# A gated mix of softmax and linear attention on one core: the linear branch's feature map taken from a copy, two of its steps and the softmax scaling on GpSimd, and a new static order

## The chip, the core and the metric

The kernel runs on one core of a Trainium2 chip. The time is device microseconds of one execution; the figure is the median of several runs. A change of time below about 0.3% can't be told from none here.

Engines are named as in the profile: PE (TensorE), ACT (ScalarE), DVE (VectorE), POOL (GpSimd), SP (SyncE, which issues DMAs here). PEld is PE's weight load.

## What is computed

The input x is 2048 x 512 (bf16). Branch A is softmax attention with 32 heads of 16, branch B linear attention with as many; a sigmoid gate per row mixes them.

```python
def _A_ref(x, wqkv, wo):                 # H = 32, Dh = 16
    q, k, v = ...                        # x @ wqkv, split by head
    scores = jnp.einsum("bhqd,bhkd->bhqk", q, k) * (Dh ** -0.5)
    p = _softmax(scores, axis=-1)
    o = jnp.einsum("bhqk,bhkd->bhqd", p, v)
    return merge_heads(o) @ wo
def _B_ref(x, wqkv, wo):
    phi = lambda t: jnp.where(t > 0, t + 1, jnp.exp(t)) + 1e-6
    pq, pk = phi(q), phi(k)
    kv = jnp.einsum("bhsd,bhse->bhde", pk, v); z = jnp.einsum("bhsd->bhd", pk)
    o = einsum("bhqd,bhde->bhqe", pq, kv) / (einsum("bhqd,bhd->bhq", pq, z) + 1e-6)
    return merge_heads(o) @ wo
g = _sigmoid((x * gate_w).sum(-1, keepdims=True))
return g * a + (1 - g) * b
```

(`merge_heads` stands for the reference's transpose and reshape.)

## The kernel before, in words

**Units and rounds.** Branch A's scores are cut into units: one head, 128 keys, 512 queries, a 128x512 tile of PSUM. There are 32 rounds of 64 units, 2048 in all: a round is a group of eight heads (`t8`, four of them), a block of 512 queries (`qc`, four) and a parity (`par`, the even or the odd four of the eight heads). The four heads of a round sit in four row strips of PE, so up to four score matmuls go side by side (tiles `KT` and `Qz`). Their value matmuls sit in four column strips and all add up in one PSUM bank, bank 7 (weights `Vp` or `Vs`, 17 columns: 16 of V and one of ones, which gives the softmax's sum).

**Two ways to take the exponential.** A pair of units in banks 0-1 or 2-3 is read by one ACT exp of 128x1024 into a `P` tile (L894) and gives one value matmul ("piece") a unit. A unit in bank 4, 5 or 6 is drained by DVE: one addition and a maximum write an int16 tile `Z` whose bits, read as bf16, are a rough power of two (L806 drains banks 5 and 6 together, 128x1024; L845 drains one bank alone, 128x512). POOL adds two constants to its bits (`int64_add`, L871, twice for each pair), and the three tiles, weighted by `Vp` and the two scaled copies `Vs`, together approximate the exponential: three pieces a unit. A pair takes three of 18 `Z` buffers. Which unit goes which way is decided by the planner below.

**Tasks.** Everything else is a list of tasks with a release and a due time (`TS`), most of which take one of the banks 4, 5, 6 for a projection: keys, queries and values of A (`t_k`, `t_q`, `t_v`), scaling of the value weights (`t_vs`, L1136), the gate, and branch B: 16 tiles of phi(k) (`t_phik`), from them the products `MT`, `KVbd` and the sums `Zbd`, then 16 tiles of phi(q) (`t_phiq`), the denominators (`t_den`), B's output (`t_bout`) and the final projection (`t_final`).

**The feature map** (`phi`, L1197 to L1207) takes a 128x512 projection in bank b. ACT takes the exp from PSUM into `eb` (L1202, bf16), DVE makes min(e, 1) + 1e-6 in place (L1203), and DVE reads the bank again for max(t + 1 + 1e-6, e) into `phiK` (L1204). Only then is the bank free. There are two `eb` buffers.

**The end of a round** (`aout`): DVE transposes bank 7 into `T1` (L1164), which frees the bank for the next round. After every second round (15 times; the last pair is done in another way, L1174 to L1181) DVE takes the reciprocals of the sums (L1190), multiplies `T1` by them into `T2` (L1191), and transposes `T2` into `OAT` (L1194).

**What sets the order.** Every instruction's place on its engine is fixed when the kernel is built. A planner keeps, per engine, the time at which it would be free, with a planned duration of each operation (such as 606 for L845), and takes again and again the candidate that can start first, ties broken by priorities. L1203, L1191 and L1136 carry a mark (`_Port`) by which the planner lengthens them when they would meet a POOL instruction. 129 sets of knobs, one for each 16 units issued (`PLAN`, read by `X`), shift these priorities: how long PE waits for a fourth piece (`PWN`), which banks tasks may take (`B4`), and so on. The kernel then waits on semaphores only where the data need it; each engine takes its instructions in the written order. All matmuls are recorded on L482.

Of the kernel before, what the change touches and what calls it, by code (L numbers as in the profile page):

```python
# [7 lines left out]
ACT = mybir.ActivationFunctionType  # L8
# [107 lines left out]
LAT = 53.0  # L116
LATP = 97.0
LATS = 34.0
# [22 lines left out]
def bass_gated_mix__mha_block__linear_attn_block__prompt_kernel(  # L141
# [22 lines left out]
    def spl(t):  # L164
# [10 lines left out]
    DEF = {"SKEW": 4, "DSL": 80.0, "DTOL": 500.0, "PWE": 0.0, "PWT": 0.0, "PWN": 400.0, "TPR": 620, "RIDE": 1200.0, "HP": 115.0, "HD": 115.0, "NDB": 2, "SLK": 50.0, "UEX": 0.2, "TOP": 420, "B4": 1, "ROOM": 3, "REL": 0, "BOOT": 2, "PORT": 0, "LD": 8}  # L175
    PLAN = {
        0: {"UEX": -0.3, "TPR": 720, "PWE": 50.0},
        1: {"UEX": -0.3, "TPR": 720, "PWE": 50.0},
        2: {"UEX": -0.3, "TPR": 720, "PWE": 50.0, "HD": 300.0},
        3: {"UEX": -0.3, "TPR": 720, "PWE": 50.0, "HD": 300.0},  # L180
        4: {"UEX": -0.3, "TPR": 720, "PWE": 50.0, "HD": 60.0},
        5: {},
        6: {},
        7: {"UEX": -0.3, "TPR": 720, "PWE": 50.0},
        8: {"UEX": -0.3, "TPR": 720, "PWE": 50.0, "DSL": 0.0, "PWN": 200.0, "DTOL": 1000.0, "REL": 1.0, "ROOM": 4, "SLK": -100.0},
        9: {"REL": 1.0},
        10: {"REL": 1.0},
        11: {"REL": 0.5, "HD": 300.0, "PWN": 200.0, "ROOM": 1, "DSL": 0.0, "RIDE": 600.0},
        12: {"REL": 1.0, "HD": 300.0, "PWN": 200.0, "ROOM": 1, "DSL": 0.0, "RIDE": 600.0, "PWE": 100.0, "B4": 0},
        13: {"REL": 1.0, "HD": 0.0, "PWN": 200.0, "ROOM": 1, "DSL": 0.0, "RIDE": 600.0, "PWE": 100.0, "B4": 0},  # L190
        14: {"REL": 1.0},
        15: {"REL": 1.0, "PWN": 600.0},
        16: {"REL": 1.0, "PWN": 600.0},
        17: {"REL": 1.0, "HP": 220.0, "PWT": 400.0},
        18: {"REL": 1.0, "HP": 220.0, "PWT": 400.0},
        19: {"REL": 1.0, "HP": 160.0, "PWT": 400.0},
        20: {"REL": 1.0, "HP": 160.0, "PWT": 400.0},
        21: {"REL": 1.0, "HP": 160.0, "PWT": 400.0},
        22: {"REL": 1.0, "HP": 220.0, "PWT": 400.0, "PWE": 100.0, "B4": 2},
        23: {"REL": 0.5, "HP": 160.0, "PWT": 400.0, "PWN": 200.0},  # L200
        24: {"REL": 0.5, "HP": 160.0, "PWT": 400.0, "PWN": 200.0, "DTOL": 0.0, "HD": 200.0},
        25: {"REL": 1.0, "PWN": 600.0, "B4": 2},
        26: {"REL": 1.0, "PWE": 50.0, "DTOL": 0.0, "DSL": 300.0},
        27: {"REL": 1.0, "HP": 220.0, "PWT": 400.0, "HD": 60.0, "PWE": 200.0},
        28: {"REL": 1.0, "HP": 220.0, "PWT": 400.0, "HD": 60.0, "PWE": 200.0, "B4": 2},
        29: {"REL": 1.0, "HP": 220.0, "PWT": 400.0, "HD": 60.0, "PWE": 50.0},
        30: {"REL": 1.0, "HP": 220.0, "PWT": 400.0, "UEX": 1.0, "SKEW": 2},
        31: {"REL": 1.0, "HP": 220.0, "PWT": 400.0, "UEX": 1.0, "SKEW": 2, "RIDE": 300.0},
        32: {"REL": 1.0, "HP": 220.0, "UEX": 1.0, "HD": 60.0, "SKEW": 2, "RIDE": 900.0, "PORT": 1, "PWE": 100.0, "DSL": 300.0},
        33: {"REL": 1.0, "HP": 220.0, "PWT": 250.0, "UEX": 1.0, "HD": 200.0, "SKEW": 2, "RIDE": 900.0, "PWE": 100.0, "DSL": 300.0, "PWN": 600.0},  # L210
        34: {"HP": 160.0, "PWT": 250.0, "RIDE": 600.0, "PWN": 900.0, "SKEW": 2, "DSL": 0.0},
        35: {"SKEW": 0, "TPR": 450},
        36: {"SKEW": 0, "TPR": 450},
        37: {"SKEW": 0, "TPR": 560, "ROOM": 2, "PWN": 200.0, "HD": 200.0, "DSL": 150.0, "PWE": 200.0},
        38: {"SKEW": 0, "TPR": 560, "ROOM": 2, "PWN": 200.0, "HD": 200.0, "DSL": 150.0, "PWE": 200.0},
        39: {"REL": 1.0, "HP": 220.0, "PWT": 250.0},
        40: {"UEX": -0.3, "TPR": 720, "PWE": 50.0, "DSL": 0.0, "PWN": 200.0, "DTOL": 1000.0, "REL": 1.0, "ROOM": 4, "SLK": -100.0, "PWT": 400.0, "HP": 160.0},
        41: {"UEX": -0.3, "TPR": 720, "PWE": 50.0, "DSL": 0.0, "B4": 0, "PWN": 200.0, "DTOL": 1000.0, "REL": 1.0, "ROOM": 4, "SLK": -100.0, "PWT": 400.0, "HP": 160.0, "PORT": 1, "SKEW": 2},
        42: {},
        43: {"UEX": -0.3, "TPR": 560, "PWE": 50.0, "DSL": 0.0, "PWN": 200.0, "DTOL": 1000.0, "REL": 1.0, "ROOM": 1, "SLK": -100.0, "PWT": 250.0, "HP": 160.0, "PORT": 1, "SKEW": 2},  # L220
        44: {"UEX": -0.3, "TPR": 560, "PWE": 50.0, "DSL": 0.0, "PWN": 200.0, "DTOL": 1000.0, "REL": 1.0, "ROOM": 1, "SLK": -100.0, "PWT": 250.0, "HP": 160.0, "PORT": 1, "SKEW": 2},
        45: {"UEX": -0.3, "TPR": 560, "PWE": 50.0, "DSL": 0.0, "PWN": 200.0, "DTOL": 1000.0, "REL": 1.0, "ROOM": 1, "SLK": 0.0, "NDB": 1, "PWT": 250.0, "HP": 160.0, "PORT": 1, "SKEW": 2},
        46: {},
        47: {},
        48: {},
        49: {"HP": 160.0},
        50: {"HP": 160.0},
        51: {"HP": 160.0, "B4": 0, "SKEW": 1, "DTOL": 1000.0, "HD": 200.0},
        52: {"HP": 160.0},
        53: {"HP": 160.0, "DTOL": 1000.0},  # L230
        54: {"UEX": -0.3, "TPR": 720, "PWE": 50.0, "HD": 60.0},
        55: {"UEX": -0.3, "TPR": 720, "PWE": 50.0, "HD": 60.0, "SKEW": 1, "DTOL": 0.0, "DSL": 0.0},
        56: {"UEX": -0.3, "TPR": 720, "PWE": 50.0, "HD": 60.0, "SKEW": 1, "DTOL": 0.0, "DSL": 0.0, "RIDE": 300.0},
        57: {"UEX": -0.3, "TPR": 650, "PWE": 50.0, "HD": 60.0, "SKEW": 1, "REL": 1.0, "DTOL": 0.0, "DSL": 0.0, "RIDE": 300.0, "SLK": -100.0, "PWT": 100.0},
        58: {"UEX": -0.3, "TPR": 650, "PWE": 50.0, "SKEW": 1, "REL": 1.0, "DTOL": 2000.0, "DSL": 0.0, "RIDE": 300.0},
        59: {"HP": 160.0, "SKEW": 1},
        60: {"HP": 160.0, "SKEW": 1, "PWE": 50.0, "DTOL": 2000.0, "UEX": -0.3},
        61: {"REL": 1.0, "PWN": 600.0, "B4": 2, "DTOL": 2000.0},
        62: {"REL": 1.0, "PWN": 600.0, "B4": 2, "PWT": 250.0},
        63: {"REL": 1.0, "B4": 2, "HD": 200.0, "PWT": 250.0, "ROOM": 2},  # L240
        64: {"REL": 1.0, "B4": 2, "HD": 200.0, "PWT": 250.0, "ROOM": 2},
        65: {},
        66: {"UEX": -0.3, "TPR": 720, "PWE": 50.0},
        67: {"UEX": -0.3, "TPR": 720, "PWE": 50.0, "HD": 300.0, "RIDE": 300.0, "B4": 2},
        68: {"UEX": -0.3, "TPR": 650, "PWE": 50.0, "HD": 300.0, "RIDE": 300.0, "B4": 2, "ROOM": 2, "PWN": 600.0, "DTOL": 2000.0},
        69: {"UEX": -0.3, "TPR": 650, "PWE": 50.0, "HD": 300.0, "RIDE": 300.0, "B4": 2, "ROOM": 2, "PWN": 600.0, "DTOL": 2000.0, "REL": 0.5},
        70: {"REL": 1.0, "B4": 2, "HD": 200.0, "PWT": 250.0, "ROOM": 2, "HP": 160.0},
        71: {"REL": 1.0, "B4": 2, "HD": 200.0, "PWT": 250.0, "ROOM": 2, "HP": 160.0, "RIDE": 600.0},
        72: {"REL": 1.0, "B4": 2, "HD": 200.0, "PWT": 250.0, "ROOM": 2, "HP": 160.0, "RIDE": 2500.0, "UEX": 0.6},
        73: {"REL": 1.0, "PWN": 600.0, "B4": 2, "HD": 60.0, "PWT": 250.0, "ROOM": 2, "HP": 220.0, "RIDE": 2500.0},  # L250
        74: {"REL": 1.0, "PWN": 200.0, "B4": 2, "HD": 60.0, "PWT": 250.0, "HP": 220.0, "RIDE": 2500.0, "TPR": 650, "SLK": 0.0},
        75: {"REL": 1.0, "PWN": 200.0, "HD": 60.0, "PWT": 250.0, "HP": 220.0, "RIDE": 2500.0, "TPR": 650, "SLK": 0.0},
        76: {"REL": 1.0, "PWN": 200.0, "HD": 60.0, "PWT": 250.0, "HP": 220.0, "RIDE": 600.0, "TPR": 650, "SLK": 0.0, "SKEW": 1},
        77: {"UEX": -0.3, "TPR": 650, "PWE": 50.0, "HD": 60.0, "SKEW": 1, "TOP": 800, "REL": 1.0, "DTOL": 0.0, "DSL": 0.0, "RIDE": 300.0, "SLK": -100.0, "PWT": 100.0},
        78: {"UEX": 0.6, "TPR": 650, "PWE": 50.0, "HD": 60.0, "SKEW": 1, "TOP": 800, "REL": 1.0, "DTOL": 1000.0, "DSL": 0.0, "RIDE": 300.0, "SLK": -100.0, "PWT": 100.0},
        79: {"ROOM": 1, "PWN": 900.0, "REL": 1.0, "SKEW": 0},
        80: {"ROOM": 1, "PWN": 200.0, "REL": 1.0, "SKEW": 0, "DSL": 0.0, "HP": 220.0, "TPR": 650},
        81: {"REL": 1.0, "PWN": 600.0, "B4": 2, "DTOL": 2000.0, "PWT": 100.0},
        82: {"REL": 1.0, "B4": 0, "DTOL": 2000.0, "PWT": 100.0},
# [1372 lines left out]
```

## Time and profile before

| | |
|---|---|
| median of 3 runs | 655.76 us (655.49 to 657.0) |
| profiled execution | span 653.0 us from its first to its last instruction, granted TensorE clock 1.000; its time is not given apart from the span |
| ACT exps of scores (L894) | 664 of 128x1024: 1328 units |
| DVE drains (L806, L845) | 301 pairs and 118 singles: 720 units |
| POOL adds (L871) | 726, 437.5 us busy |
| feature map, 32 tiles | L1202 21.8 us on ACT; L1203 9.6 and L1204 22.0 us on DVE |
| normalisation, 15 times | L1191 12.3 us, L1190 5.1, L1194 10.5, all on DVE |
| scaling of value weights (L1136) | 32 times, 0.244 to 0.740 us, 14.5 us |

How to read it: a row of the groups gives line, engine, operation, output <- input, shapes and count, then busy time, the mean length of one in ns, and the engine's idle time just before them with what ended it. Busy times on PE are the union of overlapping matmuls in flight. On DVE, ACT and PE an instruction's length overlaps the next one's beginning, so the distance between two starts is what one takes of the engine. The chain is the sequence of work that ended last. In a timeline, the columns are start, length, engine, line, operation, tiles and count, and in brackets the idle time before it and what ended it.

### The profile page before, as it was taken

How to read it: one execution, taken by the hardware profiler on the slowest of the kernel's cores; microseconds unless marked ns; L12 is line 12 of the kernel's file. 1: busy time of each engine (PE TensorE's matmuls, PEld its weight loads, DVE VectorE, ACT ScalarE, POOL GpSimd, SP SyncE). 2: the span in 40 equal slices, each digit the busy share in tenths (PEclk: the TensorE clock that was granted, in tenths of full speed). 3: DMA queues.
4: the chain of work that ended last, by engine and by line, in shares of the span. 5: the costliest groups of instructions: out<-in, count | busy, mean ns of one | idle time of the engine just before them, and what ended most of it. 6: DMA issues, size and time to landing. Idle time of an engine off the chain costs nothing.

```text
span 653.0 us, 20046 instructions
## 1 busy us (share of the span) xinstructions
PE 631.8 (97%) x8601; PEld 191.1 (29%) x8601; DVE 582.2 (89%) x723; ACT 633.0 (97%) x706; POOL 442.7 (68%) x744
## 2 busy tenths in 40 slices
PE   8999999999999999999999999999999999999998
PEld 4422232322222223233333223222222222222224
DVE  6899989898798998899889899889999898998994
ACT  5899999999999999999999999999999999999995
POOL 4376576676687787676666456668678786877683
PEclk9999999999999999999999999999999999999999
DMA  7610001000100000000101000000000000001001
GB/s 162 188 27 4 8 1 34 2 2 11 34 10 2 2 15 6 11 2 2 34 9 26 19 11 9 14 21 16 20 10 19 26 18 26 10 17 27 17 3 34
DMA packets 33072, 14.82 MB, mean 23 GB/s; under 512 B 24404, under 2 KB 32980, under 8 KB 32984
## 3 DMA queue, kind: packets, MB, share of 16 engines
q1 hardware_dynamic: 31640, 13.01, 8.3%
q8 instruction: 69, 1.13, 0.7%
q10 hardware_dynamic: 1344, 0.52, 0.3%
q14 instruction: 19, 0.16, 0.1%
HBM read 6.30 MB, written 2.11 MB: 13 GB/s over the span
## 4 chain that ended last, share of the span: by engine, by line
ACT 48%; PE 45%; DVE 4%; issue 1%; DMA 1%; ACTq 0%
ACT P L894 46%; PE ps L482 45%; ACT eb L1202 2%; DVE Z L806 2%; DMA wA<-in_A_wqkv_dram 1%; DVE T L1164 1%; DVE Z L845 0%; DVE Zbd L1236 0%; DVE OBn L1298 0%; ACTq L466 0%; PE ps L1060 0%; DVE outt L1339 0%; DVE eb L1224 0%; DVE QT L1105 0%; ACT P L1337 0%
## 5 line engine op out<-in xcount | busy, mean ns | idle before, releaser
L894 ACT ACTIVATE P<-ps 128x1024 bf16<-128x1024 f32 x664 | 618.3, 1122 | 6.5 <-PE ps L482 6.1
L871 POOL INT64_ADD Z<-Z x726 | 437.5, 618 | 196.5 <-DVE Z L806 181.8
L806 DVE TENSOR_SCALAR Z<-ps 128x1024 int16<-128x1024 f32 x301 | 366.6, 1218 | 46.6 <-PE ps L482 43.6
L482 PE MATMUL ps<-Qz,KT 32*128 32x512 bf16 x2048 | 261.5, 384 | 12.4 <-ACT P L894 6.4
L482 PE MATMUL ps<-Z,Vs 128*17 128x512 bf16 x1440 | 232.6, 382 | 0.0
L482 PE MATMUL ps<-P,Vp 128*17 128x512 bf16 x1328 | 229.7, 382 | 1.3 <-DVE T L1164 0.6
L482 PE MATMUL ps<-Z,Vp 128*17 128x512 bf16 x720 | 162.4, 382 | 1.0 <-DVE T L1164 0.8
L482 PEld LDWEIGHTS ps<-Qz,KT 32*128 32x128 bf16 x2048 | 67.7, 91 | 265.4 <-ACT P L894 191.4
L845 DVE TENSOR_SCALAR Z<-ps 128x512 int16<-128x512 f32 x118 | 79.9, 678 | 1.0 <-PE ps L482 0.8
L482 PEld LDWEIGHTS ps<-P,Vp 128*17 128x17 bf16 x1328 | 51.3, 88 | 63.0 <-issue 39.2
L482 PEld LDWEIGHTS ps<-Z,Vs 128*17 128x17 bf16 x1440 | 51.4, 88 | 48.5 <-issue 28.2
L482 PEld LDWEIGHTS ps<-Z,Vp 128*17 128x17 bf16 x720 | 36.0, 88 | 16.1 <-issue 8.4
L482 PE MATMUL ps<-xT,wA 128*32 128x512 bf16 (+1 forms) x544 | 37.8, 370 | 1.8 <-DMA wA<-in_A_wqkv_dram 0.9
L1164 DVE STREAM_TRANSPOSE T<-ps 128x512 f32<-128x512 f32 x32 | 22.7, 708 | 4.0 <-PE ps L482 4.0
L1204 DVE SCALAR_TENSOR_TENSOR phiK<-ps,eb 128x512 bf16<-128x512 f32 x32 | 22.0, 688 | 0.9
L1202 ACT ACTIVATE eb<-ps 128x512 bf16<-128x512 f32 x32 | 21.8, 680 | 0.0
L482 PE MATMUL ps<-wA,xT 128*32 128x256 bf16 x512 | 21.2, 275 | 0.0
L482 PE MATMUL ps<-wB,OAT 128*32 128x512 bf16 x256 | 20.2, 383 | 0.0
L482 PE MATMUL ps<-wB,xT 128*32 128x512 bf16 x256 | 19.4, 383 | 0.0
L482 PE MATMUL ps<-wB,xnat 128*32 128x512 bf16 x256 | 19.1, 382 | 0.3 <-DVE Z L845 0.2
L482 PE MATMUL ps<-xT,wB 128*32 128x512 bf16 x256 | 19.3, 383 | 0.0
L482 PE MATMUL ps<-phiK,xnat 128*32 128x512 bf16 x256 | 19.2, 382 | 0.0
(79 smaller groups left out, 230.0 us busy)
## 6 DMA issues: line engine op xcount, KB each, us to landing
Qz<-QT SPq DMA_DIRECT2D x120, 16.0 KB, 1.8
wB<-in_B_wqkv_dram SPq DMA_DIRECT2D x3, 512.0 KB, 6.3
out_dram<-outt SPq DMA_DIRECT2D x12, 128.0 KB, 1.7
wA<-in_A_wqkv_dram SPq DMA_DIRECT2D x10, 128.0 KB, 2.7
xnat<-in_A_x_dram SPq DMA_DIRECT2D x2, 512.0 KB, 8.0
xnat<-in_A_x_dram SPq DMA_DIRECT2D x6, 128.0 KB, 3.4
wB<-in_B_wo_dram SPq DMA_DIRECT2D x1, 512.0 KB, 3.7
wB<-in_A_wo_dram SPq DMA_DIRECT2D x1, 512.0 KB, 3.8
```

What stands on the lines that cost most here:

```text
L482: return lambda: nc.tensor.matmul(o, lhsT=l, rhs=r, start=start, stop=stop, skip_group_check=True)
L806: res.append(C(DV, 400, 1135, lambda: nc.vector.tensor_scalar(Z[:, zs[0], :], bank(5, 2), ZB, 0.0, op0=ALU.add, op1=ALU.max), [r_bank[5], ...
L845: res.append(C(DV, prio, 606, lambda b=b, z=z, h=h: nc.vector.tensor_scalar(Z[:, z, 512 * h:512 * (h + 1)], bank(b), ZB, 0.0, op0=ALU.add, ...
L871: return C(PO, 300, 160 + 0.416 * (hi - lo), lambda: nc.gpsimd.int64_add(Z[:, zw, lo:hi].bitcast(I64), Z[:, z0, lo:hi].bitcast(I64), cst), ...
L894: return C(AC, 500, 434 * n + 42, lambda: nc.scalar.activation(P[:, slot, 0:512 * n], bank(2 * g, n), ACT.Exp, scale=ESC), [r_bank[2 * g + ...
L1164: yield dv(637, lambda: nc.vector.transpose(T1[:, par, :], bank(7)), [r_bank[7]], [r_T1[par]])
L1202: yield ac(476, lambda: nc.scalar.activation(e16, bank(b), ACT.Exp), [r_bank[b]], [r_eb[i]])
L1204: yield dv(609, lambda: nc.vector.scalar_tensor_tensor(dst_ap, bank(b), 1.0 + 1e-6, e16, op0=ALU.add, op1=ALU.max), [r_bank[b], r_eb[i]], ...
```

## The change

Five things are done at once.

1. In `phi`, DVE first copies the projection from PSUM to its place in `phiK` as bf16, and the bank is free. ACT's exp reads that copy. DVE then makes max(t, 0) of the copy in place, POOL makes min(e, 1) + 1e-6 in place in `eb`, and POOL adds the two into `phiK`. max(t, 0) + min(exp(t), 1) + 1e-6 is the same function.
2. The product `T2 = T1 * rec` of the normalisation moves from DVE to POOL.
3. The planner may drain one of two full banks 5 and 6 alone (knob `SGL`), and gives a task that holds a bank its own priority (knob `TST`).
4. Its constants for latencies, pipes and durations are a few per cent or some tens of ns different.
5. All 129 sets of knobs and all release and due times are new, so the order of instructions on every engine and the split of units between ACT and DVE are new.

```diff
-LAT = 53.0
-LATP = 97.0
-LATS = 34.0
+LAT = 54.0
+LATP = 131.0
+LATS = 0.0
...
+    PTT, PTS = 1250, 650
...
-        5: {},
+        5: {"SKEW": 6, "DTOL": 5000.0, "PWT": 250.0, "PWN": 900.0, "RIDE": 2500.0, "NDB": 1, "SLK": 0.0, "ROOM": 4, "PORT": 1, "SGL": 395.0},
...
-        PE = _Eng("pe", SEM("s_pe"), 173.0)
-        AC = _Eng("act", SEM("s_act"), 125.0)
-        DV = _Eng("dve", SEM("s_dve"), 85.0)
-        PO = _Eng("pool", SEM("s_pool"), 25.0)
+        PE = _Eng("pe", SEM("s_pe"), 180.0)
+        AC = _Eng("act", SEM("s_act"), 154.0)
+        DV = _Eng("dve", SEM("s_dve"), 82.0)
+        PO = _Eng("pool", SEM("s_pool"), -35.0)
...
             if bool(dbank[5]) != bool(dbank[6]):
                 singles.append(5 if dbank[5] else 6)
+            elif dbank[5] and X("SGL"):
+                singles.append(5 if dbank[5][1] < dbank[6][1] else 6)
...
-                if b != 4:
+                if b != 4 and dbank[11 - b]:
+                    prio = X("SGL")
+                elif b != 4:
...
+        def po(dur, fn, reads, writes):
+            return ("OP", PO, dur, fn, reads, writes, None)
...
-            yield dl(_Port(593, 465), lambda: nc.vector.tensor_tensor(t2, t1[:, :, :, 0:16], rec[:].unsqueeze(3).to_broadcast([128, 2, 16, 16]), ALU.mult),
+            yield po(PTT, lambda: nc.gpsimd.tensor_tensor(t2, t1[:, :, :, 0:16], rec[:].unsqueeze(3).to_broadcast([128, 2, 16, 16]), ALU.mult),
                      [*r_T1, r_rec], [r_T2, *r_T2h])
...
         def phi(b, dst_ap, dst_res):
+            yield dv(609, lambda: nc.vector.tensor_copy(dst_ap, bank(b)), [r_bank[b]], dst_res)
+            yield ("FREE", b)
             yield ("WAIT", lambda: phi_free[0] or phi_free[1])
             i = 0 if phi_free[0] else 1
             phi_free[i] = False
             e16 = eb[:, i, 0:256].bitcast(BF16)
-            yield ac(476, lambda: nc.scalar.activation(e16, bank(b), ACT.Exp), [r_bank[b]], [r_eb[i]])
-            yield dv(_Port(195, 70), lambda: nc.vector.tensor_scalar(e16, e16, 1.0, 1e-6, op0=ALU.min, op1=ALU.add), [r_eb[i]], [r_eb[i]])
-            yield dv(609, lambda: nc.vector.scalar_tensor_tensor(dst_ap, bank(b), 1.0 + 1e-6, e16, op0=ALU.add, op1=ALU.max),
-                     [r_bank[b], r_eb[i]], dst_res)
-            yield ("FREE", b)
+            yield ac(476, lambda: nc.scalar.activation(e16, dst_ap, ACT.Exp), dst_res, [r_eb[i]])
+            yield dl(_Port(195, 70), lambda: nc.vector.tensor_scalar(dst_ap, dst_ap, 0.0, None, op0=ALU.max), dst_res, dst_res)
+            yield po(PTS, lambda: nc.gpsimd.tensor_scalar(e16, e16, 1.0, 1e-6, op0=ALU.min, op1=ALU.add), [r_eb[i]], [r_eb[i]])
+            yield po(PTT, lambda: nc.gpsimd.tensor_tensor(dst_ap, e16, dst_ap, ALU.add), [r_eb[i], *dst_res], dst_res)
             phi_free[i] = True
...
-                    prio = t["prio"] or (X("TPR") if room else 500)
+                    prio = t["prio"] or (X("TST") if t["held"] and X("TST") else X("TPR") if room else 500)
                 elif E is AC:
                     prio = 600
+                elif E is PO:
+                    prio, mode = 310, None
```

On POOL, these new operations have priority 310 in the planner, the adds for `Z` (L871) 300. The planner's other durations that change are L806 (1135 to 1136), L845 (606 to 614), groups of scores and pieces (208 to 211 plus 3.5 for each) and projections (times 1.028).

## The prediction

> **What bounds the kernel now.** First the page's busy shares and its chain, then the costliest groups.
>
> ```profile
> PE 631.8 (97%) x8601; PEld 191.1 (29%) x8601; DVE 582.2 (89%) x723; ACT 633.0 (97%) x706; POOL 442.7 (68%) x744
> ...
> ACT 48%; PE 45%; DVE 4%; issue 1%; DMA 1%; ACTq 0%
> ...
> L894 ACT ACTIVATE P<-ps 128x1024 bf16<-128x1024 f32 x664 | 618.3, 1122 | 6.5 <-PE ps L482 6.1
> L871 POOL INT64_ADD Z<-Z x726 | 437.5, 618 | 196.5 <-DVE Z L806 181.8
> L806 DVE TENSOR_SCALAR Z<-ps 128x1024 int16<-128x1024 f32 x301 | 366.6, 1218 | 46.6 <-PE ps L482 43.6
> ```
>
> ACT and PE both show 97%, but PE's number is overlapped flight time. The ACT row decides: its 664 exps were idle before them for 6.5 us in all. In the timeline the first exp starts at 9.74 us and the last ends at 643.4; the span ends at 653.0. In between lie 664 exps at 0.917 us (a chain piece has four in 3.67) = 608.9, 32 feature-map exps at 0.48 (one begins at 112.67, the next exp at 113.15) = 15.4, the gate's and idle time. So ACT is the bound, and the time falls only when scores move from ACT to DVE (L806, L845). All 2048 score tiles ("units") are split 1328 to ACT and 720 to DVE. DVE is idle 71 us of the span; the row says why: 43.6 us of waiting for PE to refill the banks that DVE drains.
>
> The second view is the timeline of one feature-map tile of the linear branch:
>
> ```profile
> 111.64 0.62 PE L482 MATMUL ps<-wB,xT 128*32 128x512 bf16 x8
> ...
> 112.63 1.22 DVE L806 TENSOR_SCALAR Z<-ps 128x1024 int16<-128x1024 f32 x1 [0.78 <-PE ps L482]
> 112.67 0.59 ACT L1202 ACTIVATE eb<-ps 128x512 bf16<-128x512 f32 x1
> ...
> 113.78 0.28 DVE L1203 TENSOR_SCALAR eb<-eb 128x512 bf16<-128x512 bf16 x1
> ...
> 114.09 0.69 DVE L1204 SCALAR_TENSOR_TENSOR phiK<-ps,eb 128x512 bf16<-128x512 f32 x1
> ...
> 114.84 0.12 PEld L482 LDWEIGHTS ps<-wB,xT 128*32 128x32 bf16 x8 [0.19 <-DVE phiK L1204]
> ```
>
> See that its bank, first written at 110.77, is held until 114.78 (4.0 us of one of three banks), that the next projection waits for it, and that DVE stood idle 0.78 us just then.
>
> **The change, part by part.**
>
> Feature map on DVE (32 tiles): before 0.31 (113.78 to 114.09) + 0.61 (114.09 to the next at 114.70) = 0.92 us. After: a copy out of PSUM, as the KT cast at 110.04 with the next instruction at 110.64, 0.60, and a maximum in place of the form of L1203, 0.31. 0.91: nothing gained.
>
> Normalisation (15 pairs of rounds): L1191 leaves DVE. Its row is 12.3 us busy, less 0.08 each of overlap with the next instruction (1.22 long, 1.14 apart) = **11 us** freed.
>
> The bank: the copy can run when the projection ends (112.26), so it ends near 112.95 and the bank is held 2.2 us, 1.8 less, 32 times. Worth between 0 and the whole 43.6 us of DVE's waits. In the waits by window, the two stretches with feature-map tiles (50 to 170 and 320 to 475 us) hold 3.8 + 6.8 + 7.2 + 5.3 = 23.1. I take half, as two of the three banks are filled with scores either way: **11.5 us**.
>
> The order and the new right to drain one of two full banks alone: this acts on the other 20.5 us of waits. No row prices it; a worse order is as possible as a better one (-20 to +20.5). A single costs 0.62 against 0.57 per unit in a pair (1.14/2), 0.05, a tenth of a typical 0.6 to 0.8 us wait that it can fill; I take a third, **7 us**.
>
> Sum: F = 29.5 us of DVE. A unit moved costs DVE 0.58 (602 at 0.57, 118 at 0.62) and saves ACT 0.917/2 = 0.459; the shorter run also takes its length from DVE. n x (0.58 + 0.459) = 29.5, n = 28, about 650 exps instead of 664, and 28 x 0.459 = 13.0 us.
>
> PE under the new split: 56 more value pieces, four abreast at 0.215 us (109.44 to 109.65) = +3.0; 14 fewer score groups at 0.32 (109.11 to 109.43) = -4.5. Nothing.
>
> ACT's feature-map exp reads a copy in SBUF instead of PSUM. No row of any size reads SBUF on ACT; the nearest, 0.48 from PSUM and 0.59 for a 128x512 copy, bound it at -0.1 to +0.1 each, +-3 us on the bound engine. I take 0. The Trainium skill ("Perfetto Trace Analysis", Optimizing Scalar/DVE Operations) gives ScalarE's access overhead as about 93 ns for SBUF and 51 for PSUM: by it, an estimate, the exps cost 32 x 0.042 = 1.3 us more and the gain would be 11.7. No row here shows it.
>
> POOL: 32 one-input operations and 47 two-input ones on 512 elements. One input: the memset of 2048 elements took 1.81 us and affine_select 0.345 at 128 elements, 0.235 at 8, so 0.9 ns an element, 0.12 + 512 x 0.9 = 0.6; two inputs between 0.4 (the shortest add) and twice 0.6; I take 1.2, as two operands are read. 32 x 0.6 + 47 x 1.2 = 76 us, plus 14 more pairs of adds at 1.2 = 17: POOL goes to about 530, 82%. It is hidden while POOL's adds were idle 196.5 us before; without that cover the 76 us would stand on the path of the value matmuls. Ahead of the feature map's last sum on POOL's queue is its wait for DVE's maximum, and behind it the adds (L871), behind these PE's value matmuls.
>
> The maximum overwrites what the exp reads, so DVE now waits for ACT there, as L1203 did (0.3 us in all); behind it on DVE are L806 and L845. Nothing, if placed as late. SP's and ACT's DMA work is not touched.
>
> **The rivals.**
>
> *More gain.* All 43.6 us of waits go: F = 54.6, n = 52.5, 24.1 us less: 632. For it: in the undisturbed stretch 634 to 640 a pair and a single alternate without a wait. Against: banks are refilled in step with ACT's exps at 0.92 us.
>
> *No units move, or a lock eats the gain.* Today a shared resource shows between DVE and POOL:
>
> ```profile
> 59.38 1.63 POOL L871 INT64_ADD Z<-Z  x2 [0.66 <-DVE Z L806]
> ...
> 59.57 0.96 DVE L1191 TENSOR_TENSOR T<-T,rec 128x512 bf16<-128x512 f32 x1
> ```
>
> The two adds take 1.63 instead of 1.20 and DVE's product 0.96 instead of 0.68 when they meet. The weights' scaling (L1136, bf16 to bf16) ranges from 0.244 to 0.740. In the change the maximum and POOL's minimum are released by the same exp: if POOL is first each time, DVE stands up to 0.6 x 32 = 19 us, F = 10, and the gain is 4.6: 651. With the other waits unchanged as well, 655. The skill ("SBUF — State Buffer", Who interferes with whom) makes this an exclusive lock on a port pair, held for the whole instruction; the two rows agree (+0.43 and +0.28).
>
> *Slower: POOL's queue holds the adds back.* POOL takes its order as written. PE already waits for it:
>
> ```profile
> PEld ps L482 <- POOL Z L871: 26.2, 113, 0.4
> ```
>
> This is 113 times 0.23, so the adds come just in time now. If a third of the 47 two-input operations' 1.2 us goes on to PE and from there to ACT, that is 19 us; with 11 us of freed DVE used (-4.8) 670. It decides from where the stall eats the 13 us, 0.28 us for each of the 47. Against it: 18 Z buffers, three to a pair, allow six pairs in flight, some 11 us at a pair per 1.9 us.
>
> **How the numbers follow.** The sum is a difference in the profiled execution (span 653.0, 2.8 below the median of the runs, 655.76, for what lies around it); put on the median: 655.8 - 13.0 = 642.8, say 643. Chances: this forecast (637 to 650) 0.55; more gain (628 to 637) 0.12; little moves or the lock (650 to 657) 0.15; slower (660 to 680) 0.18. A difference of 0.3% is about what a measurement of this kernel can tell, 653.8 to 657.7. Of the third case 0.05 is faster, 0.07 the same, 0.03 slower: faster 0.72, same 0.07, slower 0.21. A range of 633 to 662 leaves about 0.07 below and 0.13 above; it takes in the unknown order and the +-3 of the exp.
>
> **What would show it.** Exps near 650 and DVE units near 748 (right: the mechanism; wrong: 664). L1191's 12.3 us gone from DVE; the three feature-map steps 0.60 and 0.31 on DVE. DVE's wait for PE before pairs near 25 us. POOL near 82% with two-input operations near 1.2 us. ACT's idle before exps still near 6.5 us; over 18 us, with PE's wait for POOL well over 26, is the slow rival. The maximum with a mean near 0.9 is the lock. The forecast is wrong if exps fall while ACT's idle time rises as much.

## The result, and the profile after

The changed kernel takes **1239.6 us** (median of 4 runs, 1236.8 to 1242.7), the kernel before 655.62 us beside it: 1.890 times the time, 95% interval 1.886 to 1.894. The profiled execution has a span of 1235.0 us. The forecast was 643.

The page of the changed kernel, in the order in which the page of before was read (busy shares, the PE clock's slices, the chain, the costliest groups; L899 was L894, L876 was L871, L807 was L806):

```profile
PE 722.6 (59%) x8598; PEld 188.8 (15%) x8598; DVE 584.1 (47%) x773; ACT 645.6 (52%) x700; POOL 557.3 (45%) x841
...
PEclk9965677757677678978856697657568587989879
...
PE 36%; issue 33%; POOL 15%; DVE 8%; ACT 8%; DMA 0%; ACTq 0%; POOLq 0%
...
L899 ACT ACTIVATE P<-ps 128x1024 bf16<-128x1024 f32 x658 | 624.7, 1065 | 452.9 <-PE ps L483 451.9
L876 POOL INT64_ADD Z<-Z x744 | 437.1, 602 | 349.1 <-issue 252.2
L807 DVE TENSOR_SCALAR Z<-ps 128x1024 int16<-128x1024 f32 x248 | 302.0, 1218 | 266.4 <-PE ps L483 250.8
```

DVE and ACT do nearly the work they did before (584.1 and 645.6 us for 582.2 and 633.0), POOL 115 us more, and each of the three is idle about half the time. ACT has fewer exps (658 for 664), but waited 452.9 us before them instead of 6.5. No engine is the bound. The chain has a new entry: "issue", 33%, time in which an engine waited for nothing that the profile shows. The granted clock of PE, 1.000 before, is 0.757 on average.

Whose "issue" it is, the waits of the changed kernel say (engine and line that waited, for what, us in total, times, the longest):

```profile
ACT P L899 <- PE ps L483: 451.9, 142, 28.2
PEld ps L483 <- POOL Z L876: 407.9, 152, 27.7
...
POOL Z L876 <- issue: 252.2, 43, 6.4
...
POOL eb L1215 <- issue: 156.2, 22, 7.8
...
POOL T L1200 <- issue: 90.5, 13, 7.6
...
POOL phiK L1216 <- issue: 35.5, 5, 7.8
```

Most of it is POOL's: 534.4 us in 83 pieces, 5.9 us each before an add, 7.1 each before one of the three new steps. It also stands on the chain: of the chain's 407 us of "issue" (the 33%), 396 lie directly ahead of a POOL instruction. PE waits 407.9 us for POOL's adds, and ACT for PE. The timeline of POOL shows when it happens:

```profile
81.03 1.96 POOL L1215 TENSOR_SCALAR eb<-eb 128x512 bf16<-128x512 bf16 x1 [6.98 <-issue]
88.92 0.60 POOL L876 INT64_ADD Z<-Z  x1 [5.93 <-issue]
96.66 1.14 POOL L1216 TENSOR_TENSOR phiK<-eb,phiK 128x512 bf16<-128x512 bf16 x1 [7.14 <-issue]
103.72 3.55 POOL L876 INT64_ADD Z<-Z  x6 [5.92 <-issue]
115.03 1.96 POOL L1215 TENSOR_SCALAR eb<-eb 128x512 bf16<-128x512 bf16 x1 [7.76 <-issue]
117.08 1.15 POOL L1216 TENSOR_TENSOR phiK<-eb,phiK 128x512 bf16<-128x512 bf16 x1
123.97 4.17 POOL L876 INT64_ADD Z<-Z  x7 [5.74 <-issue]
```

The gap stands wherever POOL goes from the adds to an elementwise step or back, and not between two elementwise steps (115.03, 117.08) or two adds. The view by source line has a record for it, on POOL's queue, with the count, the shortest, median and longest length in ns, and the first and last start:

```profile
L1215 POOLq MODIFY_POOL_CONFIG  x52: 1/6/18, 74.1 to 1007.2; - x52
```

Lines 876, 1200 and 1216 have 88, 26 and 10 more. That is 176, two for each of **88 changes of kind**. POOL's list of instructions in the built program has an instruction without a tile at the same 88 places, and one more at the start; it is named `PseudoReloadLibraryIndex` and carries a number, 0 ahead of the elementwise steps and 1 ahead of the adds. The records themselves are some ns long; the 6 to 7 us lie behind them. The trace of before had two such records in all, at its first `int64_add`, a small one that the kernel makes at the start (L569); the second line is from the timeline:

```profile
L569 POOLq MODIFY_POOL_CONFIG  x2: 20/20/20, 6.2 to 6.2; - x2
...
6.34 0.19 POOL L569 INT64_ADD dummy<-dummy  x1
```

There the add follows its records without a gap: a record alone does not show a price. Why it cost nothing there was not tried.

The Trainium skill ("GPSIMD Engine Reference", 2.1 Instruction dispatch) says that GpSimd's kernels can be loaded at run time, and that the first call to one just loaded pays about 6 us (5.95 measured) that no instruction of the profile shows. The 5.9 us before the adds agree with that figure, the 7.1 before the elementwise steps are longer. The page does not say which operations share what is loaded, nor that a kernel can pay it 88 times.

### The profile page after: what moved, and what is told of

It is laid out like the page before. It is cut to its first block, busy times and chain, and to the rows that moved or that the text cites. A ratio compares the mean times of both kernels' runs of the same rounds, so it can differ in the third digit from the quotient of the medians.

```text
span 1235.0 us, 20451 instructions
## 1 busy us (share of the span) xinstructions
PE 722.6 (59%) x8598; PEld 188.8 (15%) x8598; DVE 584.1 (47%) x773; ACT 645.6 (52%) x700; POOL 557.3 (45%) x841
## 4 chain that ended last, share of the span: by engine, by line
PE 36%; issue 33%; POOL 15%; DVE 8%; ACT 8%; DMA 0%; ACTq 0%; POOLq 0%
PE ps L483 36%; ACT P L899 8%; POOL Z L876 6%; POOL eb L1215 5%; DVE Z L807 4%; POOL phiK L1216 3%; DVE Z L850 2%; POOL T L1200 1%; DVE phiK L1207 1%; DVE OAT L1203 0%; DMA wA<-in_A_wqkv_dram 0%; DVE T L1173 0%; DVE rec L1199 0%; DVE QT L1114 0%; DVE KT L1098 0%
## 5 line engine op out<-in xcount | busy, mean ns | idle before, releaser
L899 ACT ACTIVATE P<-ps 128x1024 bf16<-128x1024 f32 x658 | 624.7, 1065 | 452.9 <-PE ps L483 451.9
L876 POOL INT64_ADD Z<-Z x744 | 437.1, 602 | 349.1 <-issue 252.2
L807 DVE TENSOR_SCALAR Z<-ps 128x1024 int16<-128x1024 f32 x248 | 302.0, 1218 | 266.4 <-PE ps L483 250.8
L483 PE MATMUL ps<-P,Vp 128*17 128x512 bf16 x1316 | 276.8, 440 | 148.9 <-POOL Z L876 148.6
L483 PE MATMUL ps<-Qz,KT 32*128 32x512 bf16 x2048 | 291.5, 431 | 112.0 <-DVE Z L807 54.6
L483 PE MATMUL ps<-Z,Vs 128*17 128x512 bf16 x1464 | 275.2, 436 | 132.1 <-POOL Z L876 131.9
L483 PE MATMUL ps<-Z,Vp 128*17 128x512 bf16 x732 | 206.9, 434 | 76.8 <-POOL Z L876 76.4
L850 DVE TENSOR_SCALAR Z<-ps 128x512 int16<-128x512 f32 x236 | 158.2, 682 | 119.1 <-PE ps L483 118.1
L1215 POOL TENSOR_SCALAR eb<-eb 128x512 bf16<-128x512 bf16 x32 | 62.6, 1955 | 186.6 <-issue 156.2
L1213 ACT ACTIVATE eb<-phiK 128x512 bf16<-128x512 bf16 x32 | 20.4, 639 | 123.2 <-POOL phiK L1216 114.8
L1216 POOL TENSOR_TENSOR phiK<-eb,phiK 128x512 bf16<-128x512 bf16 x32 | 36.8, 1148 | 37.7 <-issue 35.5
L1214 DVE TENSOR_SCALAR phiK<-phiK 128x512 bf16<-128x512 bf16 x32 | 10.4, 334 | 35.2 <-ACT eb L1213 35.2
L1207 DVE CAST phiK<-ps 128x512 bf16<-128x512 f32 x32 | 21.9, 684 | 10.2 <-PE ps L483 9.9
```

The costliest lines, as they stand in the source:

```text
L483: return lambda: nc.tensor.matmul(o, lhsT=l, rhs=r, start=start, stop=stop, skip_group_check=True)
L807: res.append(C(DV, 400, 1136, lambda: nc.vector.tensor_scalar(Z[:, zs[0], :], bank(5, 2), ZB, 0.0, op0=ALU.add, op1=ALU.max), [r_bank[5], ...
L850: res.append(C(DV, prio, 614, lambda b=b, z=z, h=h: nc.vector.tensor_scalar(Z[:, z, 512 * h:512 * (h + 1)], bank(b), ZB, 0.0, op0=ALU.add, ...
L876: return C(PO, 300, 160 + 0.416 * (hi - lo), lambda: nc.gpsimd.int64_add(Z[:, zw, lo:hi].bitcast(I64), Z[:, z0, lo:hi].bitcast(I64), cst), ...
L899: return C(AC, 500, 434 * n + 42, lambda: nc.scalar.activation(P[:, slot, 0:512 * n], bank(2 * g, n), ACT.Exp, scale=ESC), [r_bank[2 * g + ...
L1207: yield dv(609, lambda: nc.vector.tensor_copy(dst_ap, bank(b)), [r_bank[b]], dst_res)
```

## The experiments

Three theories. **A**: each change of kind costs POOL 6 to 7 us, and the 88 of them are the loss. **B**: POOL's added work (115 us of elementwise steps) in its queue ahead of the adds is the loss, as in the slower rival of the prediction. **C**: the new order is bad by itself.

**Copies in the place of the three steps.** Every other instruction is the same, in the same place.

```diff
-nc.gpsimd.tensor_tensor(t2, t1[:, :, :, 0:16], rec[:].unsqueeze(3).to_broadcast([128, 2, 16, 16]), ALU.mult)
+nc.gpsimd.tensor_copy(t2, t1[:, :, :, 0:16])
-nc.gpsimd.tensor_scalar(e16, e16, 1.0, 1e-6, op0=ALU.min, op1=ALU.add)
+nc.gpsimd.tensor_copy(e16, e16)
-nc.gpsimd.tensor_tensor(dst_ap, e16, dst_ap, ALU.add)
+nc.gpsimd.tensor_copy(dst_ap, e16)
```

> The changed kernel with its order kept on every engine, but POOL's three new steps replaced by plain copies of one operand of the same size (the multiplication by 1/sum, the minimum and the last sum are left out). Theory A, the change of kind on POOL: in the changed kernel POOL stands idle 5.7 to 7.8 us, put down to issue, before nearly every first instruction after a change between the adds and the elementwise steps, 534 us in all, and the instruction list has a bare instruction there. If copies need no such change, the idle time goes and the time is that of the order itself, 640 to 665 us. Theory B, POOL's added work and its queue (115 us of elementwise work ahead of the adds): the copies take about half of that and the time falls by little, over 1100. Theory C, the new order is bad by itself: about 1240.

650.83 us (649.95 to 652.65), 0.9927 of the kernel before (0.9903 to 0.9951). Its page:

```profile
PE 631.9 (97%) x8598; PEld 184.0 (28%) x8598; DVE 579.7 (89%) x773; ACT 627.0 (96%) x700; POOL 489.5 (75%) x841
...
L899 ACT ACTIVATE P<-ps 128x1024 bf16<-128x1024 f32 x658 | 610.7, 1134 | 9.6 <-PE ps L483 9.5
L876 POOL INT64_ADD Z<-Z x744 | 438.3, 607 | 134.5 <-DVE Z L807 97.4
```

POOL still has 79 extra instructions among its adds, but no time on "issue" behind its first us, and ACT's idle time is 9.6 us. C falls: the order is sound, and with copies the time is 0.7% below the old one's. B falls as far as the number and place of the steps go; the copies are shorter, 0.61 to 0.63 us against 1.05 to 1.95.

**Adds of the same kind as the steps.** The whole computation, but the adds are 32-bit `tensor_tensor` adds.

```diff
-nc.gpsimd.int64_add(Z[:, zw, lo:hi].bitcast(I64), Z[:, z0, lo:hi].bitcast(I64), cst)
+nc.gpsimd.tensor_tensor(Z[:, zw, lo:hi].bitcast(I32), Z[:, z0, lo:hi].bitcast(I32), shc[:, w - 1:w].to_broadcast([128, (hi - lo) // 2]), ALU.add)
```

> The changed kernel with its order kept, the elementwise steps real, but all 744 int64 adds made as 32-bit integer tensor_tensor adds (the same result), so that POOL runs one family of operations. Theory A: no change of kind is left. The adds get longer, some 1.1 us for 512 elements as POOL's other two-input steps, so POOL becomes the bound with 744 x 1.1 + 115 = 930 us of work: 940 to 1050 us, faster than the changed kernel although POOL works some 400 us more. Theory B: POOL has twice the work, so slower than 1240, some 1500. Theory C: 1240 or more.

906.8 us (906.29 to 907.31), lower than A's range, as the adds took less than the 1.1 us expected, and far from B's. The adds take 1.04 us instead of 0.61, POOL is busy 853.5 us (94%): it does 296 us more work than in the changed kernel, and the kernel is 333 us faster. B falls here. Two changes are left, both at the start: the small `int64_add` comes 6.1 us and the first `tensor_tensor` add 7.2 us late, each behind two such records. That the small add pays here and not in the kernel before would fit a load that stays from the execution ahead, as this kernel ends with elementwise adds and the kernel before with `int64_add`; this was not tried.

**Fifteen tiny products, and fifteen tiny memsets, in the kernel before.** One element per partition of a spare tile, after each normalisation; the order of all else is that of before.

```diff
+        def tiny():
+            r_dummy.w = PO.add(lambda: nc.gpsimd.tensor_tensor(dummy[:, 0:1], dummy[:, 0:1], dummy[:, 0:1], ALU.mult), (r_dummy.w,))
...
+            yield ("FLAG", lambda: [tiny() for _ in range(1)])
             yield ("FLAG", lambda: flags.add(("norm", r // 2)))
```

> The kernel before with its order kept, plus 15 products of one element per partition on POOL, on a spare tile, one at the end of each normalisation; nobody waits for them. Theory A: 15 x 2 changes of kind at 6 to 7 us of POOL each, 200 us on POOL; POOL had 210 us of idle time and the Z buffers cover a part, so +60 to +200: 715 to 855 us. Theory B: 15 x 0.1 us of work, 656 to 660. Theory C says nothing of it: 656.

831.2 us (829.3 to 832.59), 1.268 times the kernel before (1.2653 to 1.2707). Its POOL rows:

```profile
L871 POOL INT64_ADD Z<-Z x726 | 430.5, 608 | 268.1 <-DVE Z L806 164.0 <-issue 88.2 <-DVE Z L845 12.7
L1161 POOL TENSOR_TENSOR dummy<-dummy 128x1 f32<-128x1 f32 x15 | 2.9, 192 | 106.9 <-issue 106.9
```

2.9 us of work that nobody waits for cost 176 us: 195 us of gaps (7.1 to the product, 5.9 back), of which the idle time and the `Z` buffers that my slower rival counted on covered a tenth. A holds, at the upper end of its range.

With `nc.gpsimd.memset(dummy[:, 0:1], 0.0)` in the same place:

> As the run with 15 tiny products, but each is a memset of the same element, which followed the adds without a gap at the start of the kernel before. Theory A: no change of kind, 655 to 658. Theory B: the same work as the tiny products, so the same time as they give. Theory C: 656.

656.28 us, 1.0008 of the kernel before (0.9996 to 1.002): no difference. So it is the kind of operation, not an interruption of the adds: neither memsets nor copies, standing among the adds, cost a change, and the elementwise arithmetic does.

**Three products in a row** at each of the 15 places (`range(3)`):

> As the run with 15 tiny products, but three of them in a row at each of the 15 places: 45 products, the same 30 changes of kind. Theory A1, the price is one of changing kind: as with 15, 828 to 838 us. Theory A2, every elementwise instruction on POOL carries a price of its own: about 175 us more for each 15, so 1150 to 1200.

840.96 us (838.0 to 843.91), 3 us above A1's range: 30 products more cost 10 us, not 350. The price is one of changing kind (A1), and falls once for a group.

**The two parts by themselves.** From the run with copies, only the product of the normalisation is made real again, then only the two steps of the feature map:

> The changed kernel with its order kept; only the 15 products of the softmax scaling are real on POOL, the feature map's two steps are copies (the minimum and the sum are left out). The instruction list has 30 bare instructions ahead of changes of kind (15 products, each with the way back). Theory A: 651 as with copies alone + 15 x 11.7 us, the price of a detour by the tiny products = 826; 790 to 850. Theory B (the work of the products): 15 x 0.45 us more than the copies, so 651 to 660.

> The changed kernel with its order kept; only the feature map's 64 POOL steps are real, the 15 products of the softmax scaling are copies (the scaling by 1/sum is left out). Theory A: 64 changes of kind, 32 detours at 11.7 us + 1.9 us a tile by which the two steps are longer than copies: 651 + 375 + 60 = 1086; 1000 to 1120. With the products alone the sum of both excesses should come near the changed kernel's 589 us. Theory B: 651 + 60 at most, 711.

815.6 us (814.75 to 816.45) and 1100.16 us (1098.29 to 1102.03), both in A's ranges. The table takes each excess over the copies' 650.83 us (for the tiny products, over the kernel before beside them), less what the real steps run longer than copies (0.44 us for the scaling; 1.32 and 0.53 for minimum and sum, 1.86 a tile; the whole length of the added products in the last row), divided by the changes, two records each. That the longer steps stand in the time at their whole length was assumed, not tried:

| run | changes of kind | excess, us | less longer steps | us per change |
|---|---|---|---|---|
| the change | 88 | 588.8 | 523 | 5.9 |
| feature map alone | 64 | 449.3 | 390 | 6.1 |
| scaling alone | 30 | 164.8 | 158 | 5.3 |
| tiny products, on the kernel before | 30 | 176.0 | 176 | 5.9 |
| three in a row, on the kernel before | 30 | 184.8 | 179 | 6.0 |

Five runs with two orders and 30 to 88 changes give nearly one price, 5.3 to 6.1 us. The two parts together (614) are a little more than the whole (589), which saves six changes by steps that stand next to each other. The run with the scaling alone also shows that a copy goes with either kind, after the adds as after a product:

```profile
72.65 2.38 POOL L876 INT64_ADD Z<-Z  x4 [6.08 <-issue]
74.98 0.60 POOL L1215 COPY eb<-eb 128x512 bf16<-128x512 bf16 x1
...
115.97 1.05 POOL L1200 TENSOR_TENSOR T<-T,rec 128x512 bf16<-128x512 f32 x1 [7.10 <-issue]
116.98 0.60 POOL L1216 COPY phiK<-eb 128x512 bf16<-128x512 bf16 x1
123.45 8.31 POOL L876 INT64_ADD Z<-Z  x14 [5.88 <-issue]
```

**The three steps in DVE's queue**, at the places where POOL had them; whole computation, all other instructions in their order (the planner counts them as POOL's, and they are added to DVE's list):

```diff
+            ev = DV.add(fn, deps_of(DV, reads, writes))
...
-                fin = emit(c.E, c.dur, c.fns, c.reads, c.writes, name=c.name)
+                if c.E is PO and not c.name.startswith("shift"):
+                    fin = emit_on_dve(c.dur, c.fns, c.reads, c.writes)
+                else:
+                    fin = emit(c.E, c.dur, c.fns, c.reads, c.writes, name=c.name)
```

> The changed kernel, whole computation, order of all other instructions kept, but the three POOL steps stand in DVE's queue at the places where POOL had them; POOL runs its adds alone. Theory A: no change of kind is left, so nothing of the 585 us stays except what the steps cost DVE: 32 x (0.3 + 0.3 to 0.6) + 15 x 0.8 = 31 to 41 us more work on an engine that was idle 70 us in the run with copies. 651 plus up to 35: 655 to 685 us. Theory B, the work or the place of the three steps is what hurts: well over 700 us, since DVE is nearer to full than POOL.

668.98 us, 1.0207 of the kernel before (1.0184 to 1.023). DVE is busy 612.5 us, 33 more than with copies, and the time is 18 us longer: about half of the added work is hidden. With minimum and sum as one instruction, `scalar_tensor_tensor(dst_ap, e16, 1.0, dst_ap, op0=ALU.min, op1=ALU.add)`:

> As the run with the three steps in DVE's queue, but minimum and sum are one instruction, and the 1e-6 is added in the maximum: 32 x 0.6 + 15 x 0.8 = 31 us more work for DVE than with copies on POOL. Theory A: 652 to 680 us, at most 10 us below the other. If DVE's idle time hides all of it, it would be near 651 and beat both kernels. Theory B: well over 700.

667.58 us, 1.0178 (1.0154 to 1.0202): the joined step takes 0.80 us on DVE against 0.54 + 0.50. Neither beats the kernel before. A's range held both times, and with the steps off POOL nothing of the 584 us is left but what fits DVE's added work. The only run faster than the kernel before, the copies, leaves out part of the computation; no whole kernel here beats it.

## Why the prediction was wrong

**The step that failed** is POOL's: "POOL goes to about 530, 82%. It is hidden while POOL's adds were idle 196.5 us before". It priced the 79 new instructions by their running time alone. The runs showed a price that stands between instructions, 5.9 us per change of kind, 88 times, 89% of the 589 us that separate the change from its copy version; the longer steps, at their whole length, are the other 66 us. All POOL rows that the step took for comparison (memsets, affine_select, adds) were ones that follow each other without a gap; none was of the kind that the change brings in. So the estimate was made from the wrong family, and the sign in before's trace that there are families, two MODIFY_POOL_CONFIG records at the small add on L569, played no part in it. The price itself could not be read there, as that add followed without a gap. What could be counted ahead was the changes: `PseudoReloadLibraryIndex` stands once in POOL's list before and 89 times in the changed kernel's. The step's own sum was a little off too: 442.7 + 76 + 17 is 536, and POOL was busy 557.3 us.

**The slower rival** had the path right: POOL's queue holds the adds back, PE waits for POOL (26.2 us before, 407.9 after), ACT for PE. Its signs were seen too (ACT idle over 18 us: 452.9). Its price of 0.4 us for each of the 47 two-input steps was too small by far: 584 us over 47 is 12.4 each, as there were 88 changes of kind, nearly two for each of the 47. The 11 us of cover by 18 `Z` buffers, put forward against it, did not hold: the tiny products show 11.7 us lost of each 13.0.

**The rest of the forecast** can be read off the copies' run, where those terms stand without the changes of kind (its POOL steps are shorter than the real ones, and it leaves out part of the computation): 4.4 us gained (655.25 to 650.83) instead of 13.0.

- The bound and the mechanism hold there: exps fell and the time with them. 12 units moved (720 to 732), forecast 28; 12 x 0.459 = 5.5 us.
- The scaling's 12.3 us did leave DVE, and copy and maximum cost DVE about what was said: 21.8 + 11.3 us busy against 22.0 + 9.6.
- PE's 14 fewer score groups, 4.5 us less, are not shown: the score matmuls are 2048 in both kernels, and PE is busy 631.9 us in the copies' run for 631.8.
- The mis-sized term is the 18.5 us for the freed bank and the single drains. DVE's waits for PE, in the kernel before (two lines) and in the run with copies, are

```profile
DVE Z L806 <- PE ps L482: 43.6, 79, 1.3
...
DVE Z L845 <- PE ps L482: 0.8, 1, 0.8
...
DVE Z L807 <- PE ps L483: 29.3, 59, 1.1
DVE Z L850 <- PE ps L483: 7.3, 24, 0.8
...
DVE phiK L1207 <- PE ps L483: 3.2, 8, 0.9
```

  With copies that is 39.8 us, against 44.4 before: 4.6 gained. The wait went from the pairs to the singles and the new copy. And there are 236 singles instead of 118, each 0.05 us a unit dearer, 6 us. DVE is busy 89% of the span as before. How much of this is the bank and how much the order was not separated.
- The exp from the copy takes 0.52 us of ACT at the median, from its start to the next exp's (115.51 to 116.03 in the copies' run), against 0.48 from PSUM: 1.3 us for 32, where the prediction took 0. The lengths do not show it: 0.698 us at the median in the copies' run, 0.631 with the steps on DVE, where the distance is 0.52 as well, and 0.674 before. The estimate of 1.3 us that the prediction worked out from the two figures of the Trainium skill ("Perfetto Trace Analysis", Optimizing Scalar/DVE Operations) agrees with the distances.
- The two-input steps took 1.05 and 1.15 us (1.2 said). The one-input step took 1.95, not 0.6.
- The lock: the maximum was 0.309 at the median and up to 0.764 in the copies' run, 11.3 us in all where 9.9 were planned (10.4 in the changed kernel itself). If the longer ones are the lock, it costs 1 to 2 us, not 19.

PE's low clock was not in the forecast. It was below 1 in the runs in which PE is idle a fifth of the time or more: 1.000 before (PE busy 97%), 0.895 with the 15 tiny products (80%), 0.86 with the 32-bit adds (81%), 0.757 in the changed kernel (59%). Score matmuls took 0.431 us at the mean instead of 0.384. What that adds was not tried; the price per change is the same at 0.895 and at 0.757, which argues that it adds little here.

## What to carry to other kernels

Before work is moved to POOL, ask whether POOL already runs operations of another family, count the `PseudoReloadLibraryIndex` instructions in POOL's list, and find the MODIFY_POOL_CONFIG records by source line: with `int64_add` between them, elementwise arithmetic cost about 5.9 us per change of kind here, for 1 element as for 512. If several steps have to go there, put them side by side (three in a row cost nearly as one, 10 us more in all), make all of one family (906.8 us instead of 1239.6, with slower adds), or leave them on DVE (669; the kernel before takes 655.6). An operation that the trace of before doesn't hold can have a price from outside its running time as well: one tiny instance in the old order, with nobody waiting for it, measures it.

## What was not expected of the hardware

- The gap is not even: 7.1 us on average before the elementwise steps, 5.9 before the adds, and it stands even in front of a product of 0.19 us.
- On POOL, `tensor_scalar` with two operations (minimum, add) on 512 bf16 elements takes 1.95 us, longer than `tensor_tensor` with two inputs (1.15 us) and three times a copy (0.61 us).
- `tensor_tensor` on 512 32-bit integers takes 1.04 us on POOL; `int64_add` does the same bytes in 0.61 us.
- On DVE, the minimum of 512 bf16 elements took 0.535 us at the mean in the place where POOL runs its adds close by, against 0.300 in the kernel before.
